# A gated mix of attention and a feed-forward block on one core: PV tied behind a score fill, first Q by rows of wq, dense groups in halves, gate copies off VectorE, and new numbers for the kernel's own scheduler

## Chip, cores, metric

One core of a Trainium2 chip. The metric is device time in microseconds (us) of an execution; the span is the profile's, from the first to the last instruction; the granted clock is the mean share of full speed that PE's clock had. Engines: PE (TensorE matmul), PEld (its weight loads), DVE (VectorE), ACT (ScalarE), POOL (GpSimd), SP (issues DMAs).

## The reference, cut

```python
x = A_x                                        # (1, 2048, 512), bfloat16
g = sigmoid((x * gate_w).sum(-1, keepdims=True))
a = A(x)     # 32 heads of 16; 4 segments of 512 tokens: causal softmax attention inside
             # a segment, plus a linear-attention memory M, z of the earlier segments;
             # mixed by sigmoid(beta) per head; then @ wo
b = B(x)     # relu(x @ W_gate) * (x @ W_up) @ W_down, F = 1792
return g * a + (1 - g) * b
```

## The kernel before

The kernel does not write its instructions in order. It describes about a thousand operations, each with an estimated duration, a priority key and buffers from pools, and a small list scheduler of its own (run while the program is built) puts them in one order; where an operation may run on either of two engines, it picks the engine as well. Each engine then runs its own part of that order, strictly in order, waiting on semaphores. So a duration in this file costs nothing on the chip, but it decides the order (and, for copies that DVE or ACT may do, the engine), and an order that comes of wrong durations makes engines wait.

```python
MM = 0.216
def op(self, name, engs, emit, deps=(), key=0.0, cls=1, mode=None, alloc=(), uses=(), land=0.0): ...
    # engs: {"DVE": 0.62} is the engine and the estimated time; mode: D dense, R fill, C PV
# ... in run(), what PE takes next (penalties keep PV next to other work of mode C):
k = o.key
if o.mode == "C":
    k += 4.0 if mode == "D" else -20.0
```

PSUM has one score tile S of four banks and four single banks G for everything else. PE has three kinds of work, of which PV is the product of the softmax weights with V:

```python
# D: a dense group of four 128x512 matmuls (projections, gate, up); down and output likewise
def mm4(g, lhs, rhs):
    def f(e):
        for ci in range(NC):
            nc.tensor.matmul(g.t[:], lhsT=lhs(ci), rhs=rhs(ci), start=(ci == 0), stop=(ci == NC - 1))
    return f
# R: a score fill, four heads at once in four row strips of the array; then exp on ACT, mask on POOL
nc.tensor.matmul(sp.t[:, j, off:off + w], lhsT=ks[rows, kb * P:(kb + 1) * P],
                 rhs=QT[s, c].t[rows, q0:L], start=True, stop=True, tile_position=(32 * j, 0))
nc.scalar.activation(eb_.t[:], sp.t[:], ACT.Exp, scale=SCALE)
# C: PV, four heads at once in four column strips
nc.tensor.matmul(g.t[32 * j:32 * j + 32, L - w:L], lhsT=Vp[s].t[:, kb, h * HP:h * HP + 32],
                 rhs=src.t[:, j, off:off + w], start=(kb == 0), stop=(kb == 3), tile_position=(0, 32 * j))
```

There are 16 units (segment, group of 8 heads) of five fills and two PV each. S is single, so a fill waits until the exp of the fill before it (1.88 us) is done; dense work fills PE in between. The keys say when each is wanted:

```python
TA0, PU = 9.0, 15.0                 # unit i is wanted at TA0 + i * PU (us)
kf = k0 + n * PU / 5                # fill n of a unit
key=k0 + (3 + 2 * r) * PU / 5       # PV r of a unit
```

The gate values are replicated by small copies, 16 for each of the four segments, priced at 1.1 us together:

```python
for j in range(4):
    for k in range(4):
        nc.vector.tensor_copy(R[s][32 * j:32 * j + 32, :, k], rcol[32 * k:32 * k + 32, cols])
b = op(f"R{s}", {"DVE": 1.1}, f, deps=[a], key=kz + 4)
```

The softmax here doesn't subtract the row's maximum and nothing guards it: scores larger than these inputs give would overflow.

Of the kernel before, what the change touches and what calls it, by code (L numbers as in the profile page):

```python
# [7 lines left out]
BF16 = mybir.dt.bfloat16  # L8
# [4 lines left out]
P = 128  # L13
# [141 lines left out]
def kernel(  # L155
# [42 lines left out]
    hTp = pool("hT", 18, [P, L])  # L198
# [6 lines left out]
    Ep = pool("E", 8, [P, 4, L])  # L205
# [18 lines left out]
    def c_zero(e):  # L224
        nc.vector.memset(zero[:], 0.0)
# [33 lines left out]
    def c_dummy(e):  # L259
        for _ in range(10):  # L260
            nc.tensor.matmul(g_dummy.t[:], lhsT=zero[:, 0:P], rhs=zero[:], start=True, stop=True)  # L261
    g_dummy = Buf(G)
    o_dummy = op("dummy", {"PE": 3.4}, c_dummy, deps=[o_zero], key=-1000, mode="D", alloc=[g_dummy])
# [19 lines left out]
    for t in range(4):  # L283
        def f(e, t=t):
            nc.sync.dma_start(out=xn[0].t[:, t, :], in_=x[t * P:(t + 1) * P, :])
        lx0.append(load(f"x0_{t}", f, 131072, 0, alloc=[xn[0]] if t == 0 else [], uses=[] if t == 0 else [xn[0]]))
# [7 lines left out]
    lw["wq"] = loadw("wq", wq_sb, A_wq, 0, D, -200, eng="ACT")  # L294
# [42 lines left out]
    for t in range(4):  # L337
        g = Buf(G)

        def f(e, t=t, g=g):  # L340
            gv = g.t[:].bitcast(BF16)
            for c in range(NC):
                nc.tensor.transpose(gv[:, c * P:(c + 1) * P], xn[0].t[:, t, c * P:(c + 1) * P], ident[:])  # L343
        a = op(f"xtr{t}", {"PE": 0.3}, f, deps=[lx0[t], o_ident], key=-500, mode="D", alloc=[g], uses=[xn[0]])

        def f(e, t=t, g=g):
            gv = g.t[:].bitcast(BF16)[:, 0:512].rearrange("p (c q) -> p c q", c=NC)
            dst = xT[0].t[:, :, t * P:(t + 1) * P]
            if e == "DVE":
                nc.vector.tensor_copy(dst, gv)  # L350
            else:
                nc.scalar.activation(dst, gv, ACT.Copy)
        xc0.append(op(f"xcp{t}", {"DVE": 0.45, "ACT": 0.6}, f, deps=[a], key=-500, cls=0,
                      alloc=[xT[0]] if t == 0 else [], uses=[g] + ([] if t == 0 else [xT[0]])))
# [7 lines left out]
    TA0, PU = 9.0, 15.0  # L362
# [22 lines left out]
    o_hg = op("hg", {"DVE": 1.4}, f, deps=[o1], key=12)  # L385
# [6 lines left out]
    for s in range(NSEG):  # L392
        kz = TA0 + 4 * PU * s - (0 if s == 0 else 25)
        zo = []
        for t in range(4):
            def f(e, s=s, t=t):
                nc.vector.tensor_tensor_reduce(  # L397
                    out=xn[s].t[:, t, :], in0=xn[s].t[:, t, :], in1=gwrep[:], scale=1.0, scalar=0.0,
                    op0=ALU.mult, op1=ALU.add, accum_out=zg[:, 4 * s + t:4 * s + t + 1])
            zo.append(op(f"z{s}{t}", {"DVE": 0.62}, f, deps=xn_dep[s] + [lgw] + (xc0 if s == 0 else []), key=kz + t, cls=2, uses=[xn[s]]))  # L400
# [4 lines left out]
        a = op(f"zc{s}", {"DVE": 0.08}, f, deps=zo, key=kz + 4)  # L405
# [5 lines left out]
        def f(e, s=s, cols=cols):  # L411
            for j in range(4):
                for k in range(4):
                    nc.vector.tensor_copy(R[s][32 * j:32 * j + 32, :, k], rcol[32 * k:32 * k + 32, cols])  # L414
        b = op(f"R{s}", {"DVE": 1.1}, f, deps=[a], key=kz + 4)
# [11 lines left out]
        o_ng[s] = op(f"ng{s}", {"DVE": 0.2}, f, deps=[a], key=kz + 6, cls=2)  # L427
# [4 lines left out]
    o_m2 = {}  # L432
# [3 lines left out]
    def mm4(g, lhs, rhs):  # L436
        def f(e):
            for ci in range(NC):
                nc.tensor.matmul(g.t[:], lhsT=lhs(ci), rhs=rhs(ci), start=(ci == 0), stop=(ci == NC - 1))  # L439
        return f  # L440
# [8 lines left out]

    def proj_q(s, c):  # L450
        g, q = Buf(G), Buf(QTp)
        QT[s, c] = q
        a = op(f"q{s}{c}", {"PE": 4 * MM},
               mm4(g, lambda ci: wq_sb[:, ci, c * P:(c + 1) * P], lambda ci: xT[s].t[:, ci, :]),
               deps=xr[s] + [lw["wq"]], key=dkey(4), mode="D", alloc=[g, q], uses=[xT[s]])
# [5 lines left out]
    def phi(name, src, dep, store, kk, pl, etp, key):  # L461
# [10 lines left out]
        return op(name + "b", {"DVE": 0.65}, f, deps=[a], key=key, cls=1, alloc=[dst], uses=[src, et])  # L472
# [3 lines left out]
    def proj_k(s, c):  # L476
        g, k, ko = Buf(G), Buf(KTp), Buf(KOp)
        KT[s, c], KO[s, c] = k, ko
        a = op(f"k{s}{c}", {"PE": 4 * MM},
               mm4(g, lambda ci: wk_sb[:, ci, c * P:(c + 1) * P], lambda ci: xT[s].t[:, ci, :]),  # L480
               deps=xr[s] + [lw["wk"]], key=dkey(4), mode="D", alloc=[g, k], uses=[xT[s]])
# [18 lines left out]
    def proj_v(s, t):  # L500
        g = Buf(G)
        if t == 0:
            Vp[s] = Buf(Vpp)
        a = op(f"v{s}{t}", {"PE": 4 * MM},
               mm4(g, lambda ci: xT[s].t[:, ci, t * P:(t + 1) * P], lambda ci: wv_sb[:, ci, :]),
               deps=xr[s] + [lw["wv"]], key=dkey(4), mode="D", alloc=[g], uses=[xT[s]])
# [4 lines left out]
                       alloc=[Vp[s]] if t == 0 else [], uses=[g] + ([] if t == 0 else [Vp[s]]))  # L511

    def mz(s, c):
# [17 lines left out]
        b = op(f"mza{s}{c}", {"DVE": 0.25}, f, deps=[a, o_mzacc[c]], key=a.key, cls=0, uses=[g])  # L531
# [6 lines left out]
        o_m2[s, c] = o_mzacc[c] = op(f"m2{s}{c}", {"DVE": 0.25}, f, deps=[b, o_bdm, prev], key=a.key, cls=1)  # L538
# [5 lines left out]
    def gu(s, fb):  # L544
        g, u, rg, h = Buf(G), Buf(G), Buf(rgp), Buf(hTp)
        hT[s, fb] = h
        a = op(f"g{s}.{fb}", {"PE": 4 * MM},
               mm4(g, lambda ci: wg_sb[:, ci, fb * P:(fb + 1) * P], lambda ci: xT[s].t[:, ci, :]),
               deps=xr[s] + [lwg[fb], (gu_prev[0], 0.0) if gu_prev[0] else None], key=dkey(4), mode="D",
               alloc=[g], uses=[xT[s]])  # L550
        b = op(f"u{s}.{fb}", {"PE": 4 * MM},
               mm4(u, lambda ci: wu_sb[:, ci, fb * P:(fb + 1) * P], lambda ci: xT[s].t[:, ci, :]),
               deps=xr[s] + [lwu[fb], (a, 0.0)], key=dkey(4), mode="D", alloc=[u, h], uses=[xT[s]])
# [13 lines left out]
    def dn(s, t):  # L567
        g, ob = Buf(G), Buf(osp)
        tt = 4 * s + t
        prev = None  # L570
        for p0, p1 in ((0, 4), (4, 8), (8, 11), (11, 14)):
            def f(e, p0=p0, p1=p1):
                for fb in range(p0, p1):
                    nc.tensor.matmul(g.t[:], lhsT=hT[s, fb].t[:, t * P:(t + 1) * P], rhs=wd_sb[:, fb, :],  # L574
                                     start=(fb == 0), stop=False)
            gate = late[s, t] if p0 == 0 else []
            prev = op(f"d{s}{t}.{p0}", {"PE": (p1 - p0) * MM}, f,
                      deps=[lwd, (prev, 0.0) if prev else None] + gate + [o_h[s, fb] for fb in range(p0, p1)],
                      key=dkey(p1 - p0), mode="D", alloc=[g] if p0 == 0 else [],
                      uses=([] if p0 == 0 else [g]) + [hT[s, fb] for fb in range(p0, p1)])  # L580

        def f(e):
            for c in range(NC):
                nc.tensor.matmul(g.t[:], lhsT=oT[s, c].t[:, t * P:(t + 1) * P], rhs=wo_sb[:, c, :],  # L584
                                 start=False, stop=(c == NC - 1))
        a = op(f"wo{s}{t}", {"PE": 4 * MM}, f, deps=[lwo, (prev, 0.0)] + [o_oT[s, c] for c in range(NC)],
               key=dkey(4), mode="D", uses=[g] + [oT[s, c] for c in range(NC)])

        def f(e):
            if e == "DVE":  # L590
                nc.vector.tensor_scalar(ob.t[:], g.t[:], ngcol[:, tt:tt + 1], None, ALU.mult)
            else:
                nc.scalar.activation(ob.t[:], g.t[:], ACT.Copy, scale=ngcol[:, tt:tt + 1])  # L593
        b = op(f"os{s}{t}", {"DVE": 0.75, "ACT": 0.7}, f, deps=[a, o_ng[s]], key=a.key, cls=0, alloc=[ob], uses=[g])

        def f(e):
            nc.sync.dma_start(out=outf[tt * P:(tt + 1) * P, :], in_=ob.t[:])
        op(f"st{s}{t}", {"SP": 0.1}, f, deps=[b], key=a.key, cls=0, uses=[ob], land=0.4)


    fill_prev = [None]
    rec_of = {}
    units = [(s, c) for s in range(NSEG) for c in range(NC)]

    def unit(i):
# [5 lines left out]
        for n, parts in enumerate(FL):  # L611
# [20 lines left out]
            fill_prev[0] = a  # L632

# [12 lines left out]
            masks.append(m)  # L646
        pvs = []
        for r in range(2):
# [3 lines left out]
            def f(e, r=r, g=g, ea=ea, ebf=ebf, ec=ec):  # L652
                for kb, src, off, w in ((0, ea, 0, 512), (1, ebf, 0, 384), (2, ec, 256 * r, 256), (3, ebf, 384, 128)):
# [7 lines left out]
                   deps=[masks[3 * r], masks[3 * r + 1], masks[2]] + [o_v[s, t] for t in range(4)],  # L661
                   key=k0 + (3 + 2 * r) * PU / 5, mode="C", alloc=[g], uses=[ea, ebf, ec, Vp[s]])
            pvs.append((a, g))
        recs = []
        if s > 0:
            for r in range(2):
# [5 lines left out]
                a = op(f"rec{s}{c}.{r}", {"PE": MM}, f, deps=[o_pq[s, c], o_m2[s - 1, c]],  # L672
# [4 lines left out]
        if c == 0:  # L677
            o_rg[s] = (op(f"RG{s}", {"DVE": 0.4}, frg, deps=[b, o_hg] + attn_of_seg[s - 2] if s > 1 else [b, o_hg],
                          key=kz + 6, cls=2), None, None)
        org = o_rg[s][0]  # L680
        outs = []
        for kind, lst in ((0, pvs), (1, recs)):
# [4 lines left out]
            for r, (a, g) in enumerate(lst):  # L687
                def f(e, T=T, g=g, r=r):
                    nc.vector.transpose(T.t[:, r, :, :].rearrange("p b e -> p (b e)"), g.t[:])  # L689
                tr.append(op(f"tr{s}{c}.{kind}{r}", {"DVE": 0.65}, f, deps=[a] + tr, key=k0 + PU * 0.8, cls=0,  # L690
# [36 lines left out]
    def proj(s):  # L727
        for c in range(NC):
            proj_q(s, c)
            proj_k(s, c)  # L730
        for t in range(4):
            proj_v(s, t)
# [72 lines left out]
```

## Time and profile before

| | before |
|---|---|
| device time, median of 4 runs | 294.06 us (three fast ones 290.39 to 294.24; the fourth took 943.99) |
| profiled execution | 291.03 us, span 289.0 us, granted clock 1.000 |
| PE / DVE / ACT / POOL busy | 95 / 70 / 74 / 32 % |

From the page of the kernel before: the span, the busy times, PE's busy tenths in 40 slices, and the chain that ended last, by engine.

```profile
span 289.0 us, 5294 instructions
PE 274.0 (95%) x2050; PEld 111.0 (38%) x2050; DVE 203.3 (70%) x484; ACT 213.4 (74%) x204; POOL 93.6 (32%) x141
PE   8999788999969999999999999999999999996995
PE 82%; DVE 11%; ACT 3%; issue 3%; POOL 0%; POOLq 0%; ACTq 0%; DVEq 0%
```

PE is the limit nearly everywhere. Its busy share hides two losses, though, because the ends of matmuls are modelled. The timeline shows both when it is read from start to start. First lines of PE from 36.8 us (start, length, engine, line, what, count, idle time before and who ended it):

```profile
36.80 1.03 PE L439 MATMUL G<-xT,wg_sb 128*128 128x512 bf16 x4
37.76 0.39 PE L625 MATMUL S<-QT,KO 32*128 32x512 bf16 x4
38.08 1.04 PE L439 MATMUL G<-xT,wu_sb 128*128 128x512 bf16 x4
...
41.69 0.40 PE L625 MATMUL S<-QT,KO 32*128 32x384 bf16 x8
43.88 1.02 PE L439 MATMUL G<-xT,wg_sb 128*128 128x512 bf16 x4 [1.79 <-DVE hT L561]
```

A dense group followed by dense work takes 0.86 us (four times 0.216); followed by a fill it takes 0.96 us, and the fill, which streams for 0.21 us, takes 0.32 us. So every change of mode loses about 0.11 us. The Trainium skill, "TensorEngine Tiling (Array Packing)", Key Properties, says that "Changing tiling mode (not just tile) drains the TensorE"; the trace agrees, and gives the price. The last line is the second loss, a wait of 1.79 us for DVE. Here is DVE at that time:

```profile
39.36 0.64 DVE L561 TENSOR_TENSOR hT<-G,rg 128x512 bf16<-128x512 f32 x1
39.93 3.17 DVE L414 COPY R<-rcol 32x4 f32<-32x4 f32 x16
43.13 0.69 DVE L561 TENSOR_TENSOR hT<-G,rg 128x512 bf16<-128x512 f32 x1
```

The product that PE waits for stands, in DVE's order, behind sixteen gate copies. They took 3.17 us where the scheduler counted 1.1. The waits at 32 and 80 us stand behind the same sixteen copies of other segments (3.14 us from 28.22 us, 3.60 us from 78.17 us). Near the end PE waits for exp instead, because no dense work is left that may run yet:

```profile
263.38 0.59 PE L670 MATMUL G<-pq,M 128*128 128x512 bf16 x2
264.69 0.29 PE L625 MATMUL S<-QT,KT 16*128 16x256 bf16 x4 [0.72 <-ACT E L635]
...
267.07 0.40 PE L625 MATMUL S<-QT,KO 32*128 32x512 bf16 x4 [1.97 <-ACT E L635]
```

And what PE waited for in sum (us, times, longest):

```profile
PE G L439 <- DVE hT L561: 3.5, 2, 1.8
PE S L625 <- ACT E L635: 2.7, 2, 2.0
PE G L518 <- DVE hT L561: 2.0, 1, 2.0
PE G L518 <- DVE mzacc L528: 0.8, 1, 0.8
```

### The profile page before, as it was taken

Reading aid. Unit: us, or ns where it says so; the run is one execution under the profiler, and the core shown is the slowest. Engines: PE = TensorE matmul, PEld = TensorE weight load, DVE = VectorE, ACT = ScalarE, POOL = GpSimd, SP = SyncE. Lnnn points to the kernel's source line nnn. Section 1 sums busy time; section 2 is a strip of 40 time slices with the busy share of each in tenths; the row PEclk is TensorE's granted clock in tenths of the full one; section 3 lists DMA queues with packets and bytes.
Section 4 is the critical chain, followed back from the end, with each engine's and each line's share of the span. In section 5 each row is a group of like instructions: output and inputs, shape, how many; then the busy total and the mean of one; then the engine's idle time right before and its main releaser. Section 6 shows DMA issues by size and latency. Waiting matters only on the chain.

```text
span 289.0 us, 5294 instructions
## 1 busy us (share of the span) xinstructions
PE 274.0 (95%) x2050; PEld 111.0 (38%) x2050; DVE 203.3 (70%) x484; ACT 213.4 (74%) x204; POOL 93.6 (32%) x141
## 2 busy tenths in 40 slices
PE   8999788999969999999999999999999999996995
PEld 4344234433333333433334343333433433332442
DVE  1598999977699954999969372879766452948240
ACT  3799576989857587899877658798877776778502
POOL 8233332322225332233325232333324232332210
PEclk9999999999999999999999999999999999999999
DMA  7998970001800010001200100000000010000002
GB/s 234 308 221 255 345 149 0 3 18 40 163 0 20 19 37 2 0 3 36 20 18 3 36 20 18 0 2 1 2 0 0 20 36 22 0 2 0 1 2 73
DMA packets 26745, 15.42 MB, mean 53 GB/s; under 512 B 13536, under 2 KB 26720, under 8 KB 26720
## 3 DMA queue, kind: packets, MB, share of 16 engines
q1 hardware_dynamic: 26192, 14.56, 19.9%
q10 hardware_dynamic: 528, 0.52, 0.5%
q8 instruction: 16, 0.26, 0.4%
q14 instruction: 9, 0.07, 0.1%
HBM read 9.84 MB, written 2.10 MB: 41 GB/s over the span
## 4 chain that ended last, share of the span: by engine, by line
PE 82%; DVE 11%; ACT 3%; issue 3%; POOL 0%; POOLq 0%; ACTq 0%; DVEq 0%
PE G L439 43%; PE G L574 15%; PE S L625 8%; PE G L656 6%; PE G L584 5%; DVE R L414 3%; ACT E L635 3%; DVE hT L561 3%; DVE xn L397 2%; PE G L261 2%; PE G L670 1%; DVE T L689 1%; PE G L343 0%; POOL E L642 0%; DVE O L703 0%
## 5 line engine op out<-in xcount | busy, mean ns | idle before, releaser
L635 ACT ACTIVATE E<-S 128x2048 bf16<-128x2048 f32 x80 | 150.0, 1875 | 38.8 <-PE S L625 36.1
L642 POOL TENSOR_SCALAR_AFFINE_SELECT E<-E 128x512 bf16<-128x512 bf16 x128 | 86.2, 688 | 181.3 <-ACT E L635 176.1
L439 PE MATMUL G<-xT,wu_sb 128*128 128x512 bf16 x224 | 57.8, 380 | 1.8 <-DVE hT L561 1.7
L439 PE MATMUL G<-xT,wg_sb 128*128 128x512 bf16 x224 | 57.7, 380 | 1.8 <-DVE hT L561 1.8
L561 DVE TENSOR_TENSOR hT<-G,rg 128x512 bf16<-128x512 f32 x56 | 38.0, 681 | 29.8 <-PE G L439 19.0
L689 DVE STREAM_TRANSPOSE T<-G 128x512 f32<-128x512 f32 x56 | 39.2, 705 | 23.4 <-PE G L656 22.9
L574 PE MATMUL G<-wd_sb,hT 128*128 128x512 bf16 x224 | 53.6, 380 | 0.0
L557 ACT ACTIVATE rg<-G 128x512 bf16<-128x512 f32 x56 | 33.2, 597 | 8.0 <-PE G L439 7.7
L439 PEld LDWEIGHTS <-wg_sb 128*128 128x128 bf16 x224 | 20.4, 98 | 27.5 <-issue 5.8
L439 PEld LDWEIGHTS <-wu_sb 128*128 128x128 bf16 x224 | 19.5, 98 | 27.3 <-issue 7.8
L574 PEld LDWEIGHTS <-hT 128*128 128x128 bf16 x224 | 20.1, 98 | 25.4 <-issue 4.3
L656 PE MATMUL G<-E,Vp 128*32 128x256 bf16 (+3 forms) x512 | 23.6, 302 | 0.5 <-DVE T L689 0.2
L703 DVE TENSOR_TENSOR O<-T,sm 128x512 bf16<-128x512 f32 x28 | 21.7, 776 | 0.4
L593 ACT ACTIVATE os<-G,ngcol 128x512 bf16<-128x512 f32 x12 | 8.2, 687 | 15.0 <-PE G L584 13.9
L625 PE MATMUL S<-QT,KO 32*128 32x256 bf16 (+3 forms) x256 | 17.1, 300 | 2.0 <-ACT E L635 2.0
L656 PEld LDWEIGHTS <-Vp 128*32 128x32 bf16 x512 | 10.8, 96 | 19.1 <-issue 11.0
L625 PE MATMUL S<-QT,KT 16*128 16x512 bf16 (+3 forms) x256 | 17.3, 302 | 0.9 <-ACT E L635 0.7
L439 PE MATMUL G<-xT,wq_sb 128*128 128x512 bf16 x64 | 16.5, 380 | 0.6 <-DVE xT L350 0.6
L439 PE MATMUL G<-xT,wk_sb 128*128 128x512 bf16 x64 | 16.5, 380 | 0.0
L584 PE MATMUL G<-wo_sb,oT 128*128 128x512 bf16 x64 | 16.2, 380 | 0.0
L439 PE MATMUL G<-wv_sb,xT 128*128 128x512 bf16 x64 | 15.7, 380 | 0.0
L397 DVE CUSTOM_DVE_ANT_0 xn<-xn,gwrep 128x512 bf16<-128x512 bf16 x16 | 11.8, 756 | 2.9 <-DMA wg_sb<-in_B_W_gate_dram 2.9
(68 smaller groups left out, 209.6 us busy)
## 6 DMA issues: line engine op xcount, KB each, us to landing
out_dram<-os SPq DMA_DIRECT2D x16, 128.0 KB, 1.7
wd_sb<-in_B_W_down_dram SPq DMA_DIRECT2D x1, 1792.0 KB, 12.2
xn<-in_A_x_dram SPq DMA_DIRECT2D x3, 512.0 KB, 5.0
wg_sb<-in_B_W_gate_dram SPq DMA_DIRECT2D x2, 512.0 KB, 5.4
wu_sb<-in_B_W_up_dram SPq DMA_DIRECT2D x2, 512.0 KB, 6.6
wg_sb<-in_B_W_gate_dram SPq DMA_DIRECT2D x3, 256.0 KB, 6.6
wu_sb<-in_B_W_up_dram SPq DMA_DIRECT2D x3, 256.0 KB, 6.2
wq_sb<-in_A_wq_dram ACTq DMA_DIRECT2D x1, 512.0 KB, 4.2
```

What stands on the lines that cost most here:

```text
L397: nc.vector.tensor_tensor_reduce(out=xn[s].t[:, t, :], in0=xn[s].t[:, t, :], in1=gwrep[:], scale=1.0, scalar=0.0, op0=ALU.mult, op1=ALU.ad ...
L439: nc.tensor.matmul(g.t[:], lhsT=lhs(ci), rhs=rhs(ci), start=(ci == 0), stop=(ci == NC - 1))
L557: nc.scalar.activation(rg.t[:], g.t[:], ACT.Relu)
L561: nc.vector.tensor_tensor(h.t[:], u.t[:], rg.t[:], ALU.mult)
L574: nc.tensor.matmul(g.t[:], lhsT=hT[s, fb].t[:, t * P:(t + 1) * P], rhs=wd_sb[:, fb, :], start=(fb == 0), stop=False)
L584: nc.tensor.matmul(g.t[:], lhsT=oT[s, c].t[:, t * P:(t + 1) * P], rhs=wo_sb[:, c, :], start=False, stop=(c == NC - 1))
L625: nc.tensor.matmul(sp.t[:, j, off:off + w], lhsT=ks[rows, kb * P:(kb + 1) * P], rhs=QT[s, c].t[rows, q0:L], start=True, stop=True, tile_po ...
L635: nc.scalar.activation(eb_.t[:], sp.t[:], ACT.Exp, scale=SCALE)
L642: nc.gpsimd.affine_select(out=v, in_=v, compare_op=ALU.is_ge, fill=0.0, base=0, pattern=[[0, 4], [1, P]], channel_multiplier=-1)
L656: nc.tensor.matmul(g.t[32 * j:32 * j + 32, L - w:L], lhsT=Vp[s].t[:, kb, h * HP:h * HP + 32], rhs=src.t[:, j, off:off + w], start=(kb == 0 ...
L689: nc.vector.transpose(T.t[:, r, :, :].rearrange("p b e -> p (b e)"), g.t[:])
L703: nc.vector.tensor_tensor(O.t[:].rearrange("p b r e -> p r b e"), T.t[:, :, :, 0:DH], sm.t[:, 1][:, :, :, None].to_broadcast([P, 2, 16, DH ...
```

## The change

Its intent: fewer changes of mode (PV right behind a fill), finer pieces for the scheduler (dense groups in halves), an earlier start (Q while x and wq are still landing), less work on DVE (gate copies on POOL), DVE durations as measured, and attention paced faster, so that dense work is left for the end. Core of the diff:

```diff
-    hTp = pool("hT", 18, [P, L])
+    hTp = pool("hT", 22, [P, L])
-    Ep = pool("E", 8, [P, 4, L])
+    Ep = pool("E", 7, [P, 4, L])
-        for _ in range(10):                 # warm-up matmuls, of zeros
+        for _ in range(5):                  # of ones
# x of the first segment in two column halves, wq in two row halves; x transposed by column
# block; Q of all four head groups accumulated in the four banks of S, one row block at a time:
+    for ci in range(NC):
+            for c in range(NC):
+                nc.tensor.matmul(qS.t[:, c, :], lhsT=wq_sb[:, ci, c * P:(c + 1) * P], rhs=xT[0].t[:, ci, :],
+                                 start=(ci == 0), stop=(ci == NC - 1))
-    TA0, PU = 9.0, 15.0
+    TA0, PU = 7.0, 14.0
-                nc.vector.tensor_tensor_reduce(     # x * gate_w, summed
+                nc.vector.scalar_tensor_tensor(
-        b = op(f"R{s}", {"DVE": 1.1}, f, deps=[a], key=kz + 4)        # 16 copies on nc.vector
+            b.append(op(f"R{s}{j}", {"POOL": 0.8}, f, deps=[a], key=kz + 4, cls=2))   # 4 of 16, nc.gpsimd
-    def mm4(g, lhs, rhs):
+    def dense(name, g, lhs, rhs, deps, alloc, uses):      # two operations of two matmuls each
# twelve DVE durations are set anew; one of them, cut:
-            a = op(f"pr{s}{c}.{kind}", {"DVE": 0.62}, ...
+            a = op(f"pr{s}{c}.{kind}", {"DVE": 0.80}, ...
+            if n == 1 and pending[0] is not None:         # n: the fill of the next unit
+                rest(*pending[0], a)                      # PV and what follows it
-                   key=k0 + (3 + 2 * r) * PU / 5, mode="C", ...
+                   ([(pvs[0][0], 0.0)] if r else [(behind, 0.0)] if behind else []),
+                   key=k0 - 100, mode="C", ...
# down projection in pairs of matmuls; the last output tile in two column halves
```

## The prediction

> **What bounds the kernel.** TensorE. The page shows a span of 289.0 us, PE busy 95%, DVE 70%, ACT 74%, POOL 32%, full clock; the chain that ended last is 82% PE. The timeline of PE, read start to start, gives its sum:
>
> - dense matmuls (projections, gate/up, down, output, recall), 952 of 128x512: 0.216 us each, 205.5 us
> - score fills and PV: 17.1 us each; memory update and transposes 3.6 us
> - every change between dense, fill (row strips) and PV (column strips) loses about 0.12 us (a dense group ahead of a fill takes 0.96 us instead of 0.86). PE's order shows 221 such changes: 26 us. The Trainium skill, "TensorEngine Tiling (Array Packing)", Key Properties, says that changing the tiling mode drains the engine; the trace agrees with 0.12 us.
> - waits, about 10 us: 1.7 and 1.8 us at 32 and 42 us and 2.0 us at 80 us (released by the DVE product hT), 0.8 us at 47 us, and 2.7 us at 264-267 us, where fills wait for exp. The table by stage shows DVE busy 17.7 of 18.0 us from 32 to 50 us: DVE holds that stage.
> - the start: PE's first useful work at 5.5 us; the end: 3.3 us behind the last matmul.
>
> **What the change does, costed.**
>
> 1. PV of a unit, both halves, right behind the second fill of the next. The order of instructions shows runs of one mode falling from 222 to 190: 32 x 0.12 = 3.9 us, on the critical path. The surest term.
> 2. Attention is paced at 14 us a unit instead of 15 and dense work kept for the end: 98 dense matmuls (21 us) follow the last PV instead of 44. The fills that waited for exp at 264-267 us should have dense work between them: 2.5 us.
> 3. The replicated gate values (64 copies, 12.8 us of DVE, half of it between 28 and 43 us) go to POOL. DVE gets the slack that PE waited for at 32-50 us. With the scheduler's durations now near the measured ones (O product 0.80 against 0.776), fewer dense groups are placed before their buffers are free. Of about 7 us of such waits 4 should go.
> 4. First Q by rows of wq into the score banks, x in column halves: 30 dense matmuls instead of 16 stand before the first fill, which should start 1 us later than 11.25 us: net gain 1.5 us. It could be less, since only five warm-up matmuls run: the trace shows 0.43 us for a 512-column matmul until 5.5 us. The skill, "TensorE: Matmul & The Clock Gate", Part 1, says that the slow clock lasts until about 3.4 us of activity; here the transposes sped up at 6.6 us.
> 5. The last output tile in halves: 0.5 us.
> 6. Dense groups in halves, hT 22 instead of 18: nothing by themselves.
>
> Sum: 12.4 us; I take 1.2 us off for new waits. Span about 278 us; the runs lie 5.2 us above the profiled span: **283.0 us**, 279.0 to 288.5 eight times in ten. Faster by over 2%: 0.83; within: 0.15; slower: 0.02.
>
> **What would show it.** 1: 190 runs of one mode at 0.12 us. 2: no PE wait on exp after 260 us. 3: DVE under 95% from 30 to 50 us, PE waits on hT under 3 us, POOL up by about 10 us. 4: first fill near 12 us, behind 30 dense matmuls.
>
> **What would make it wrong.** POOL copies delaying the masks, and with them PV, now fixed in its place; the first projections at half clock for several us; POOL copies slower than DVE's 0.2 us; waits that only move.

## The result

| | before | after |
|---|---|---|
| device time, median | 294.06 us (4 runs) | 276.78 us (4 runs, 276.69 to 277.57) |
| ratio | | 0.9458 (95%: 0.937 to 0.9546) |
| profiled span, clock | 289.0 us, 1.000 | 275.1 us, 0.999 |
| PE waits of over 0.45 us | 10.3 us | 0.0 us |
| runs of one mode; loss at their changes | 222; 25.0 us | 190; 21.7 us |

All outputs are right. A ratio is the mean time of one kernel's runs over that of the other's of the same rounds, so not quite the ratio of the medians. Executions over 1.5% slower than the fastest of the same kernel are left out of the means. The last two rows come from PE's timeline: from the start of each run of matmuls of one mode to the start of the next, less the columns it streams (0.216 us for 512 dense columns). What is over 0.45 us counts as a wait less 0.12 us for the change itself, the rest as the loss of the change. The count takes the memory update and the transposes of x as a kind of work of their own; by the shape of the tiles alone (full array, row strips, column strips) there are 214 runs before and 180 after.

The same lines of the page of the changed kernel:

```profile
span 275.1 us, 5253 instructions
PE 265.1 (96%) x2028; PEld 114.0 (41%) x2063; DVE 197.6 (72%) x431; ACT 207.1 (75%) x194; POOL 107.7 (39%) x205
PE   5999999999999999999999999999999999999995
PE 91%; DMA 4%; ACT 2%; issue 1%; DVE 1%; ACTq 0%
```

(35 matmul records are missing from this trace: 2028 of 2063.) PE's row has no 6, 7 or 8 left inside. Its timeline where PV now stands, and at the last PV:

```profile
33.33 0.40 PE L661 MATMUL S<-QT,KT 16*128 16x384 bf16 x8
33.66 1.27 PE L702 MATMUL G<-E,Vp 128*32 128x512 bf16 x32
...
253.94 0.73 PE L702 MATMUL G<-E,Vp 128*32 128x512 bf16 x16
254.60 1.04 PE L459 MATMUL G<-xT,wg_sb 128*128 128x512 bf16 x3
```

Two PV stand in one run of 32 matmuls behind a fill, and behind the last PV dense work goes on without a gap. Its waits, those over 0.3 us that are not put down to issue (nine of 0.16 us there are missing records), but for the first warm-up matmul's:

```profile
PE G L349 <- DMA xn<-in_A_x_dram: 1.3, 1, 1.3
PE S L661 <- ACT E L674: 0.5, 2, 0.2
```

Those on hT and mzacc are gone, and 0.5 us on exp is left of 2.7. The other belongs to the start, which gained nothing. PE's first lines, before:

```profile
1.25 4.45 PE L261 MATMUL G<-os 128*128 128x512 bf16 x10 [1.25 <-DVE os L225]
5.49 1.61 PE L343 MATMUL G<-ident,xn 128*128 128x128 bf16 x16
7.71 1.02 PE L439 MATMUL G<-xT,wq_sb 128*128 128x512 bf16 x4 [0.61 <-DVE xT L350]
```

After:

```profile
1.52 2.31 PE L261 MATMUL G<-os 128*128 128x512 bf16 x5 [1.52 <-DVE os L225]
5.11 1.03 PE L349 MATMUL G<-ident,xn 128*128 128x128 bf16 x8 [1.27 <-DMA xn<-in_A_x_dram]
6.41 1.87 PE L367 MATMUL S<-xT,wq_sb 128*128 128x512 bf16 x4 [0.26 <-ACT xT L358]
8.06 0.71 PE L349 MATMUL G<-ident,xn 128*128 128x128 bf16 x8
8.61 2.75 PE L367 MATMUL S<-xT,wq_sb 128*128 128x512 bf16 x12
```

The first four Q matmuls begin 1.3 us sooner, but at half clock (about 0.42 us each): full speed came at 6.6 us before, with ten warm-up matmuls, and at 8.3 us now, with five. The first fill starts at 11.25 us behind 16 dense matmuls before, at 14.32 us behind 30 now; less 0.216 us for each of them that is 7.80 and 7.85 us.

So the span's 13.9 us are 10.3 of waits, 3.3 of mode changes, 0.4 at the end (from the last matmul's end to the span's: 3.6 to 3.2) and nothing at the start. The medians differ by 17.3 us (that of before counts the run of 943.99 us; the means differ by 15.9). The other 3.4 are in the executions: the profiled one of before happened to take 291.03 us, and its others mostly 293 to 294 (see below).

### The profile page after: what moved, and what is told of

Read it like the earlier page. It is cut to its first block, busy times and chain, and to the rows that moved or that the text cites. A ratio compares the mean times of both kernels' runs of the same rounds, so it can differ in the third digit from the quotient of the medians.

```text
span 275.1 us, 5253 instructions
## 1 busy us (share of the span) xinstructions
PE 265.1 (96%) x2028; PEld 114.0 (41%) x2063; DVE 197.6 (72%) x431; ACT 207.1 (75%) x194; POOL 107.7 (39%) x205
## 4 chain that ended last, share of the span: by engine, by line
PE 91%; DMA 4%; ACT 2%; issue 1%; DVE 1%; ACTq 0%
PE G L459 48%; PE G L604 18%; PE S L661 9%; PE G L702 6%; PE G L615 5%; DMA pK<-pk 2%; PE G L718 2%; PE S L367 2%; DMA xn<-in_A_x_dram 2%; ACT E L674 1%; PE G L544 1%; DVE T L737 1%; PE G L349 0%; ACT xT L358 0%; DVE xn L414 0%
## 5 line engine op out<-in xcount | busy, mean ns | idle before, releaser
L604 PE MATMUL G<-wd_sb,hT 128*128 128x512 bf16 (+1 forms) x231 | 53.0, 367 | 0.8 <-issue 0.3
L584 DVE TENSOR_TENSOR hT<-G,rg 128x512 bf16<-128x512 f32 x56 | 38.2, 685 | 19.0 <-ACT rg L580 10.4
L737 DVE STREAM_TRANSPOSE T<-G 128x512 f32<-128x512 f32 x56 | 37.8, 700 | 14.9 <-PE G L702 14.6
L580 ACT ACTIVATE rg<-G 128x512 bf16<-128x512 f32 x56 | 32.5, 595 | 5.2 <-PE G L459 4.8
L604 PEld LDWEIGHTS <-hT 128*128 128x128 bf16 x238 | 22.0, 98 | 24.6 <-issue 3.6
L459 PEld LDWEIGHTS <-wu_sb 128*128 128x128 bf16 x224 | 20.5, 98 | 25.9 <-issue 3.6
L623 DVE TENSOR_SCALAR os<-G,ngcol 128x512 bf16<-128x512 f32 (+1 forms) x9 | 6.2, 689 | 21.6 <-PE G L615 20.6
L702 PE MATMUL G<-E,Vp 128*32 128x256 bf16 (+3 forms) x512 | 20.5, 301 | 0.0
L661 PE MATMUL S<-QT,KT 16*128 16x512 bf16 (+3 forms) x256 | 17.3, 302 | 0.5 <-ACT E L674 0.5
L615 PE MATMUL G<-wo_sb,oT 128*128 128x512 bf16 (+1 forms) x65 | 16.6, 366 | 0.1
L432 POOL COPY R<-rcol 32x4 f32<-32x4 f32 x64 | 14.6, 229 | 2.8 <-ACT rcol L425 0.3
L625 ACT ACTIVATE os<-G,ngcol 128x512 bf16<-128x512 f32 x8 | 5.5, 687 | 12.4 <-PE G L615 12.3
```

Of the source, the lines that this page charges most:

```text
L432: nc.gpsimd.tensor_copy(R[s][32 * j:32 * j + 32, :, k], rcol[32 * k:32 * k + 32, cols])
L580: nc.scalar.activation(rg.t[:], g.t[:], ACT.Relu)
L584: nc.vector.tensor_tensor(h.t[:], u.t[:], rg.t[:], ALU.mult)
L604: nc.tensor.matmul(g.t[:, 0:W], lhsT=hT[s, fb].t[:, t * P:(t + 1) * P], rhs=wd_sb[:, fb, cs], start=(fb == 0), stop=False)
L615: nc.tensor.matmul(g.t[:, 0:W], lhsT=oT[s, c].t[:, t * P:(t + 1) * P], rhs=wo_sb[:, c, cs], start=False, stop=(c == NC - 1))
L737: nc.vector.transpose(T.t[:, r, :, :].rearrange("p b e -> p (b e)"), g.t[:])
```

## The experiments

Theories. **Load**: PE waited because DVE was full, and moving 12.8 us of copies off it cured that. **Order**: PE waited because the scheduler planned with durations that were too short and a pace that was too slow, so it put work where its inputs were not ready, and ran out of dense work at the end. Eighteen kernels ran; PE's account for the profiled execution of each, as in the table above (where the clock was halved inside, the lost time is partly in the waits):

| run | modes | waits | changes | span | clock | median | ratio to before |
|---|---|---|---|---|---|---|---|
| before | 222 | 10.3 | 25.0 | 289.0 | 1.000 | 294.06 | |
| after | 190 | 0.0 | 21.7 | 275.1 | 0.999 | 276.78 | 0.946 |
| b_r_emit_pool | 222 | 10.0 | 25.6 | 289.8 | 0.988 | 290.93 | 0.990 |
| b_r_pool (profile slow) | 222 | 10.4 | 24.7 | 290.3 | 0.982 | 288.80 | 0.980 |
| b_dur | 223 | 4.3 | 25.7 | 283.3 | 1.000 | 287.41 | 0.977 |
| b_pace14_2 | 223 | 13.9 | 25.3 | 293.2 | 0.988 | 293.84 | 1.002 |
| b_durpace | 226 | 0.0 | 25.9 | 279.1 | 0.998 | 280.80 | 0.958 |
| b_durpace_r | 219 | 1.4 | 24.3 | 279.5 | 1.000 | 281.31 | 0.960 |
| a_r_emit_dve | 190 | 12.6 | 22.3 | 288.5 | 0.988 | 290.07 | 0.989 |
| a_r_dve | 189 | 1.4 | 21.3 | 276.4 | 0.999 | 278.57 | 0.948 |
| a_olddur_2 | 190 | 6.4 | 21.0 | 280.9 | 0.994 | 282.61 | 0.965 |
| a_pace15_2 | 185 | 8.0 | 21.3 | 284.7 | 0.988 | 286.70 | 0.979 |
| a_whole | 186 | 7.5 | 20.9 | 282.0 | 0.988 | 282.76 | 0.962 |
| a_pvfree | 213 | 1.7 | 23.4 | 278.8 | 0.999 | 281.27 | 0.959 |
| a_oldstart | 192 | 1.6 | 21.7 | 275.9 | 1.000 | 277.87 | 0.949 |
| a_dummy9 | 189 | 1.7 | 22.1 | 276.3 | 0.998 | 277.83 | 0.947 |
| best1_2 | 192 | 2.1 | 22.1 | 276.6 | 1.000 | 278.54 | 0.952 |
| best2 | 196 | 0.5 | 21.9 | 274.9 | 0.999 | 276.49 | 0.943 |

The runs that end in _2 had been submitted once before, with the same text, when no chip ran them. (The last two runs, after_again and best2_again, are at the end.)

**1. The gate copies moved, PE's order kept.** In the kernel before, one word: the copies are planned for DVE and issued on POOL.

```diff
-                    nc.vector.tensor_copy(R[s][32 * j:32 * j + 32, :, k], ...)
+                    nc.gpsimd.tensor_copy(R[s][32 * j:32 * j + 32, :, k], ...)
```

> The kernel before with one part of the change: the 64 copies of the gate values are issued on POOL instead of DVE, and PE's order stays that of before to the instruction. Load theory (PE waited at 32-50 and 80 us because DVE was full, and those copies filled it): about 7 us of PE waits on hT and mzacc shrink to under 2.5 us, span down 4 to 7 us, ratio to before 0.975 to 0.985. Order theory (the waits come from where the scheduler placed dense groups, with DVE durations below the real ones): waits shrink by under 2 us, ratio 0.993 or more. Both: the waits at 264-267 us on exp stay (2.7 us).

Ratio 0.990, waits 10.0 us instead of 10.3: neither theory's number came whole. In the list of waits those on hT and mzacc fell from 6.3 to 3.2 us, most of the way to the load theory's 2.5; two stretches at half clock (from 47.8 and 266.3 us), which the profile of before doesn't have, fill the sum up again. And the run was not clean. DVE itself then stood 4.2 us idle behind POOL's copies, since the product that needs them kept its place in DVE's order. So it was done again with the scheduler told (b_r_pool):

> The kernel before with the gate copies on POOL and the scheduler told so (in the earlier run with PE's order kept, DVE sat 4.2 us idle behind POOL's copies, in program order). PE's order has 222 runs of one mode as before. Load theory, second attempt: DVE no longer waits for POOL, PE waits between 25 and 85 us fall from 7.2 us to under 3 us, span 284 to 286 us at full clock. Order theory (freeing DVE is not enough while the scheduler's DVE durations are too short): waits of 4 us or more stay there, span 287 us or more.

The profiled execution was slow already at the start and is not used. The fast executions of these rounds had spans of 284.6 (clock 1.000), 286.1 and 288.1 us against 290.1 to 293.0 for before; 284.6 is 4.4 us under the 289.0 that before shows at full clock, and inside the load theory's 284 to 286. Moving the copies, planned for, does help the kernel before, with about 4 us, read from a single execution at full clock; both theories have a share there.

**2. The gate copies put back in the changed kernel**, with the plan kept (a_r_emit_dve: nc.gpsimd to nc.vector, still planned for POOL) and with the plan told (a_r_dve: also "POOL" to "DVE").

> The changed kernel with that part undone: the 64 copies are issued on DVE, PE's order stays that of the changed kernel. Load theory: PE waits of 4 to 7 us come back between 25 and 85 us, span 279 to 282 us. Order theory: under 2 us, span at most 277 us.

> The changed kernel with the gate copies on DVE and the scheduler told so, at 0.8 us for four, so that DVE's order is planned for them (the earlier run kept the plan made for POOL and lost 13 us). Load theory: 2 to 6 us of PE waits come back, span 277 to 281 us. Order theory (the 13 us were copies standing in DVE's order where the plan had not put them): under 1.5 us, span at most 276.6 us.

Against the plan they cost 13 us, planned for they cost 1.3 us of span (other executions up to 2.4): the same copies on the same engine. The profiled execution (276.4 us, 1.4 us of waits) just meets the order theory's numbers; two of the other three (277.3 and 277.5 us) fall into the load theory's. What the 13 us are is seen around 96 us of a_r_emit_dve, DVE first, then PE:

```profile
96.55 1.46 DVE L432 COPY R<-rcol 32x4 f32<-32x4 f32 x4
98.04 0.71 DVE L767 STREAM_TRANSPOSE oT<-O 128x512 bf16<-128x512 bf16 x1
```

```profile
94.90 0.38 PE L615 MATMUL G<-wo_sb,oT 128*128 128x512 bf16 x1
98.81 0.39 PE L615 MATMUL G<-wo_sb,oT 128*128 128x512 bf16 x1 [3.52 <-DVE rp L443]
```

The transpose oT, which PE's output projection reads, stands behind unplanned copies, and PE waits 3.52 us (the profile names DVE's next instruction; oT's end at 98.75 us is what the matmul reads). For a_r_emit_dve the order theory said at most 277 us and the load theory 279 to 282; the span was 288.5, so both were wrong in size: neither had counted that unplanned work hurts wherever it is put.

**3. Durations alone, pace alone, both, on the kernel before.** These edits change no line that issues an instruction, only the plan (b_durpace_r moves the copies too). The plan picks some engines as well, but b_durpace doesn't unload DVE by that: DVE has 482 instructions and 206.5 us of work there, against 484 and 203.3 before.

```diff
b_dur:     twelve DVE durations as in the change; gate copies {"DVE": 1.1} -> {"DVE": 3.2}
b_pace14:  -    TA0, PU = 9.0, 15.0      +    TA0, PU = 7.0, 14.0
b_durpace: both;   b_durpace_r: both, and the copies on POOL
```

> The kernel before with the scheduler's DVE durations alone set to those of the change (the gate copies, still on DVE, at their measured 3.2 us for sixteen). 223 runs of one mode. Order theory: the waits of 7.2 us between 25 and 85 us fall to under 3 us, span 285 us or less. Load theory: they stay above 5 us, span 287 us or more. The waits at the end on exp stay either way.

> The kernel before with the pace alone set to 14 us a unit from 7 us (76 dense matmuls behind the last PV instead of 44; 223 runs of one mode). Pace theory: the waits on exp at 263-267 us (about 3.2 us) go, those between 25 and 85 us (about 7 us) stay; span 285 to 287 us at full clock, up to 289 with half-clock windows. Rival: the waits at the end stay, span 288 to 292 us.

> The kernel before with two numbers of the scheduler alone: the DVE durations of the change (gate copies on DVE at 3.2 us for sixteen) and the pace of 14 us. No copy moves, PV is free, dense groups are whole, the start is the old one. PE's order has 226 runs of one mode and 50 dense matmuls behind the last PV. If durations and pace together are what removes the waits: under 2 us of waits, no half-clock window inside, span 279 to 281.5 us. If the copies on POOL, the halves or the fixed PV are needed as well: 3 us or more of waits, span 282 us or more.

> The same with the gate copies on POOL as well: 219 runs of one mode, 76 dense matmuls behind the last PV. If the copies' DVE time is what keeps a pace of 14 us from holding: waits under 1.5 us, span 278 to 280 us. If it does not matter here: the same span as the run without it, within 1 us.

Durations alone took the waits between 25 and 85 us from 7.2 to 0.8 us (here without the 0.12 us taken off each; the order theory's number) and left the waits on exp at the end. Pace alone did nothing for the time, and not as either expectation had it: the waits at the end went, but twice as many came earlier, on DVE. PE's waits in b_pace14_2, the two largest:

```profile
PE G L439 <- DVE T L689: 3.1, 2, 2.8
PE G L439 <- DVE hT L561: 2.2, 2, 1.5
```

A faster pace asks more of DVE early, and a plan that undercounts DVE cannot hold it. Both together left no wait at all, and 279.1 us of span, though DVE had no less to do. From the page of b_durpace:

```profile
span 279.1 us, 5244 instructions
PE   7999999999999999999999999999999999999995
```

So of the 17.3 us, **13 come from numbers in the scheduler alone** (294.06 to 280.80 us; 9.9 of 13.9 us in the profiled spans), with every gate copy still on DVE, PV free, dense groups whole and the old start. Moving the copies on top of that (b_durpace_r) gained nothing. The load theory falls as an explanation of this change. Its grain of truth may be that moving mis-priced work off an engine is another way to repair the plan; that is a reading of b_r_pool, not a test. No run sets the price of the gate copies alone to 3.2 us, so it stays open how much of the 13 us is theirs and how much the other twelve durations'; the twelve alone are worth 5.8 us of span in the changed kernel, where the copies are on POOL (a_olddur_2, below).

What still separates b_durpace from the changed kernel is 4.0 us of span: 36 fewer runs of one mode, 25.9 to 21.7 us of losses at their changes, 4.2 us. (The end gives 0.4 us more; the start, 7.29 us by the measure above against 7.85, takes 0.6 away.)

**4. The same two numbers taken back in the changed kernel.**

> The changed kernel with the scheduler's old, too short DVE durations (the gate copies stay on POOL). Order theory: of the DVE work that is not counted, the gate copies are gone, the rest remains (about 0.1 to 0.3 us an operation); PE waits of 1.5 to 5 us come back between 25 and 85 us, span 277 to 280.5 us. Load theory (moving the copies was enough): under 1 us, span at most 276.2 us.

> The changed kernel with attention paced at 15 us a unit from 9 us, as before. PE's order has 185 runs of one mode and 58 dense matmuls behind the last PV (98 in the changed kernel), and two fills side by side near the end with two dense matmuls ahead of them. If the pace is what took away the waits on exp at the end: 3 to 5 us of such waits come back after 245 us, span 278 to 280.5 us. Rival (the pace does nothing of its own): no such wait, span at most 275.5 us.

Old durations: 6.4 us of waits, 5.8 us of span, a little more than expected. Old pace: 9.6 us of span, far more than the 3 to 5 expected. The end of a_pace15_2 shows why (PE), with the table by stage over 6.8 us of it (busy us and instruction counts of PE, PEld, DVE, ACT, POOL; then the granted clock):

```profile
252.61 0.40 PE L661 MATMUL S<-QT,KT 16*128 16x384 bf16 x8 [1.16 <-ACT E L674]
257.42 0.40 PE L661 MATMUL S<-QT,KO 32*128 32x512 bf16 x4 [2.03 <-ACT E L674]
258.80 4.43 PE L604 MATMUL G<-wd_sb,hT 128*128 128x512 bf16 x14
270.21 0.83 PE L702 MATMUL G<-E,Vp 128*32 128x384 bf16 x12 [2.43 <-POOL E L681]
```

```profile
254.50:257.90 3.40, 1.13 (x18) 0.51 (x20) 3.33 (x8) 2.31 (x2) 1.69 (x3) 1.00 0.00 0
257.90:261.30 3.40, 3.40 (x22) 1.28 (x15) 2.84 (x6) 1.88 (x1) 1.41 (x3) 0.50 0.00 0
```

Gate and up had run out, the fills went at exp's pace, PE was busy 1.13 us of 3.40, and in the next 3.4 us its clock was halved: 14 down-projection matmuls took 4.43 us instead of about 3.2. A wait that left PE idle for two thirds of such a stretch was paid twice here.

**5. Halves, and the placing of PV.**

```diff
a_whole:  dense() issues its four matmuls as one operation again
a_pvfree: -  rest(*pending[0], a) behind fill 1 of the next unit, key k0 - 100
          +  rest(...) at the end of its own unit, key k0 + (3 + 2 * r) * PU / 5
           (the recall matmuls lose their tie to the PV before them as well)
```

> The changed kernel with dense groups of four matmuls issued whole again (PE's order has 186 runs of one mode instead of 190; output tiles still in pairs). If the halves do nothing for PE's time, as predicted: span 274 to 276 us. If the halves are what takes the waits away: waits of over 3 us, span 278 us or more.

> The changed kernel with PV placed by the scheduler again, not tied behind the second fill. Its PE order has 213 runs of one mode instead of 190. If a change of mode costs the 0.11 us that the two traces show and nothing else hangs on the placing: 23 x 0.11 = 2.5 us longer, span 277.5 us. Rival (the placing also took waits away): over 4 us longer, with waits in PE's timeline that the changed kernel does not have.

Whole groups cost 7 us of span: the waits on exp at the end come back (4.3 us in four waits; the rest of the 7.5 is half clock, for 6.8 us from 258.9 us on). The likely reason is that a fill may enter only between operations of the plan, so attention falls behind its pace; that is argued, the waits are shown. In this run output tiles still came in pairs of matmuls. My prediction had said "nothing by themselves". In the old setting halves were not needed (b_durpace has none), so they matter to this plan, not in general. PV free: 23 more runs of one mode and 1.7 us more losses at their changes, plus 1.7 us of new waits; 3.7 us of span, between the two expectations.

**6. The start.**

```diff
a_oldstart: x in rows, Q by proj_q, ten warm-up matmuls of zeros, as before; the rest as changed
a_dummy9:  -        for _ in range(5):
           +        for _ in range(9):
best1:     a_dummy9, and gate work of segment 0 behind the evacuation of Q:
           +    for o in z_first + [o_hg]:
           +        o.deps += [(o_q[0, c], None) for c in range(NC)] + [(o_k[0, 0], None)]
best2:     a_dummy9, and in mz():
           -    deps=[o_pKt[s, c]] + ...
           +    deps=[(o_pKt[s, c], 2.5)] + ...
```

> The changed kernel with the start of before: x in rows, Q in dense groups, ten warm-up matmuls of zeros. 192 runs of one mode. My prediction gave the new start 1.5 us; the two traces say 0.0 us (first fill less the dense matmuls ahead of it: 7.80 us before, 7.85 us after). If the traces are right and no wait comes of it: span 274.5 to 276.5 us. If the new start is worth its 1.5 us by another way (an earlier attention): 276.6 us or more.

> The changed kernel with nine warm-up matmuls instead of five, so that PE works until x lands at 5.1 us. If the missing gain at the start is the clock (full speed from 8.26 us after, 6.63 us before): full speed from about 6.6 us, first fill at 13.3 us instead of 14.3, span 0.7 to 1.2 us shorter than the changed kernel. Rival (it is the landing of x alone): first fill still at 14.0 us or later, gain under 0.3 us.

> A try at a better version: the changed kernel with nine warm-up matmuls and with the gate work of the first segment (which waits for DMAs landing at 10.2 us, in DVE's order ahead of the evacuation of Q) put behind that evacuation. If both readings of the start are right: full clock by 6 us, first fill at 11.5 to 12.8 us instead of 14.3 us, no wait ahead of it, and a span of 273.5 to 275.0 us. If the earlier fill is worth nothing because PE has dense work in that time anyway, and new waits appear elsewhere: 275 us or more.

> A second try at a better version: the changed kernel with nine warm-up matmuls, and with 2.5 us more allowed for the transposed keys on their way to the memory update, which PE waited 1.1 us for in the first run with nine. 196 runs of one mode. If the start is worth 0.9 us and the wait is gone: span 273.8 to 275.0 us, ratio to the changed kernel 0.997. If new waits or the six more changes of mode eat it: 275 us or more.

The old start in the changed kernel is 0.8 us of span longer, with 1.6 us of new waits: the new start is worth nothing that can be told from its side effects. Nine warm-up matmuls (a_dummy9) brought full clock at 5.7 us and let all 16 Q matmuls run by 10.6 us, 0.8 us earlier than in the changed kernel; but the first fill did not follow (14.04 us, the rival's number, though not for the rival's reason), because the evacuation of Q stood in DVE's order behind gate work that waits for DMAs landing at 10.2 us. With that moved (best1_2) the fill came at 13.25 us, not at 12, and 2.1 us of waits came up elsewhere. best2 leaves 0.5 us of them and is level with the changed kernel or a little better. To be sure, both ran on one chip in the same five rounds:

> The changed kernel itself, on the chip and in the rounds of the second try at a better version, for a comparison of like with like: span 275.0 to 275.9 us, median 276.6 to 277.6 us, as in its first run.

> The second try at a better version, beside the changed kernel. If its earlier full clock is worth what the two traces say (0.2 us of span): ratio of its mean to the changed kernel's 0.998 to 0.9995. If the 0.3 us of the first run was the chip: no difference within the spread of each.

Mean 276.60 us of six runs (276.40 to 276.91) against 277.34 (276.47 to 277.83): 0.9973, a little better than the 0.998 to 0.9995 expected; the ranges overlap. It is the fastest kernel, by 0.3%.

**Why the executions of before differ.** Of the 11 in the rounds of b_durpace, leaving out one, slow, those with a mean granted clock of 1.000 had spans of 289.1 us, with 0.994 290.3 to 290.6, with 0.988 291.3 to 292.1, with 0.982 292.4 to 292.5. (The order holds inside one chip's rounds; in those of b_r_emit_pool 1.000 came with 289.8 and 290.3 us.) In all profiles here such a mean comes of stretches of 3.4 us at half clock. The Trainium skill, "TensorE: Matmul & The Clock Gate", Part 1, describes a free-running activity window of 3.4 us and two clocks that follow from it, half and full; the traces agree with the window (3.4 us, or twice that) and with the half. They add that the edge lies near a window that is half busy. Three stretches of before's profiled execution, and one of b_r_emit_pool:

```profile
30.51:33.92 3.41, 1.72 (x9) 0.68 (x7) 3.31 (x12) 1.75 (x2) 1.87 (x2) 1.00 1.10 348
40.75:44.16 3.41, 1.61 (x18) 0.65 (x15) 3.20 (x16) 2.92 (x3) 0.66 (x2) 1.00 0.02 7
262.60:266.01 3.41, 1.77 (x14) 0.70 (x14) 3.34 (x7) 2.91 (x3) 1.23 (x2) 1.00 0.00 0
```

```profile
44.40:47.80 3.40, 1.64 (x18) 0.94 (x16) 3.40 (x10) 1.88 (x1) 1.81 (x3) 1.00 0.00 0
47.80:51.20 3.40, 3.40 (x20) 0.89 (x21) 2.19 (x10) 1.41 (x3) 0.00 (x0) 0.50 0.00 0
```

With PE busy 1.64 of 3.40 us the clock was halved next; with 1.61 to 1.77 in before's profile it was not. Before sits on the edge three times, so its executions fall on either side. Counted in every profile with clock records, window by window from its first change of clock, twelve windows at full clock were followed by half clock, with PE busy 0.60 to 1.75 us in them; none with less than 1.6 us escaped it, and none with more than 1.75 us met it (PE's ends are modelled, so the edge is no sharper than that). What it means for the other executions of before is an inference; they leave a mean clock only. Without waits there is no such stretch: every execution of the changed kernel has a mean clock of 0.998 or more.

## Why the prediction was wrong

The direction and the order of the terms held; the time, 276.78 us, lies 2.2 us under the range. Two steps failed: the size of the waits (5.3 us were to go, 10.3 went) and the offset from span to device time (5.2 us carried over, 1.7 measured). The sum had five terms, and that offset:

| term, as predicted | predicted | measured |
|---|---|---|
| 1. "32 x 0.12 = 3.9 us, on the critical path" | 3.9 | 3.3 |
| 2. and 3. waits on exp 2.5, waits on DVE 4, less "1.2 us off for new waits" | 5.3 | 10.3 |
| 4. "net gain 1.5 us" at the start | 1.5 | 0.0 |
| 5. "The last output tile in halves: 0.5 us" | 0.5 | 0.4 |
| "the runs lie 5.2 us above the profiled span" | 5.2 above | 1.7 above |

Of the 6.2 us between 283.0 and 276.78, about 2.8 are the terms (5.0 more, less 0.6, 1.5 and 0.1) and about 3.5 the offset. That the miss was no larger is luck: what the start and the changes of mode did not bring hid 2.2 us of what the waits did.

- **The waits were under-sized by 5 us.** I took 4 of 7 us for the DVE waits and gave 1.2 us back for new ones. With durations as measured and a pace of 14, none was left (changed kernel, b_durpace). I also named the wrong main carrier: "DVE gets the slack that PE waited for" credited the move of the copies, which on top of right durations and pace gains nothing (b_durpace_r). The durations stood beside it in the same term, without a share of their own; together with the pace they are enough. The pace was given 2.5 us; alone it gains nothing, and in the changed kernel it carries 9.6 us. The parts do not add: the plan holds or it does not.
- **The offset was misread, by 3.5 us.** 5.2 us was the median of other executions less the span of one. The profiled execution's own time, 291.03 us, stood beside it and gives 2.0 us. The other 3 us were, by their mean clocks, slow-clock stretches of the other executions, which go when the waits go. So a second gain was hidden in what I carried over as a constant.
- **The start** was over-sized: "It could be less, since only five warm-up matmuls run" was the right reservation. Full clock came 1.6 us later in the two profiles compared (8.3 to 10.7 us in all with five warm-up matmuls, 4.4 to 7.2 us with ten, b_r_pool's slow one left out). That is not all: with an early full clock (a_dummy9) Q was done 0.8 us sooner, but the first fill only 0.3, behind DVE's order. With both put right (best1_2) it comes, less its 28 dense matmuls, at 7.2 us, 0.6 us better than before.
- **"Dense groups in halves ...: nothing by themselves"** was wrong for this plan (a_whole, 7 us).
- **Right**: what bounds the kernel, the count and, nearly, the price of mode changes (32 runs fewer for 3.3 us; b_durpace to the changed kernel: 36 for 4.2 us), no long wait on exp after 260 us, DVE under 95% from 30 to 50 us (17.0 of 20.0 us busy, 19.6 before), POOL up (14 us). The first fill came at 14.3 us, not near 12, and it did no harm, since PE had dense work.
- The fears did not come true: POOL's copies took 186 ns at the median against 163 on DVE, and no PV waited for a mask in the changed kernel. No run isolates the other pool sizes (hT 22, E 7), the new form of x * gate_w or the output's pairs.

## What to carry to other kernels

If a kernel is ordered by its own scheduler, compare every duration it plans with to the trace before changing any instruction: here thirteen durations and a pace were worth 13 of 17 us, and neither was worth it alone (6.7 us and 0.2 between the medians). Work that an in-order engine does, but the plan does not count, can cost ten times what it costs when it is planned for (13 us against 1.3 for the same copies here), since what the critical engine waits for stands behind it. And take the difference between span and device time from one and the same execution: if the others lie higher, ask for their clock.

## What the Trainium skill lacked or had wrong

- "TensorEngine Tiling (Array Packing)", Key Properties, gives no price for the drain at a change of mode. Here it is 0.11 to 0.12 us each between full array, row strips and column strips (25.0 us in 221 changes, 8 of which are between dense work and the memory update or the transposes and keep the tile shape).
- "TensorE: Matmul & The Clock Gate", Part 1, says that the clock falls after at least one idle window, and gives as the rule that PE should have no idle gaps of over about 3.4 us. Here windows that were half busy were enough: PE busy 1.64 of 3.40 us in one (b_r_emit_pool), with a single wait of 1.76 us in it, 1.13 of 3.40 us in another (a_pace15_2).
- The same page puts the change to full speed at about 4 us of sustained matmuls, "±500ns run-to-run". Here the same ten warm-up matmuls from 1.25 us on gave full speed at 4.4 us (b_dur), 5.0 (b_durpace), 6.6 (before) and 7.2 us (b_pace14_2); five matmuls and then a wait for x gave it at 8.3 to 10.7 us over eight profiled executions.
- No page that I used gives a figure for what work costs that an in-order engine does outside the plan: the same 64 gate copies on DVE went with 12.6 us of PE waits unplanned (a_r_emit_dve) and 1.4 us planned (a_r_dve).
